# Where the token order of packed attention groups is put right: in the product's operand read, or in the copy out of PSUM

## The chip, the cores and the metric

The kernel runs on one core of one Trainium2 chip. The metric is the device time of one execution in microseconds; a set of runs is judged by its median. TensorE does the matmuls, VectorE (DVE) and ScalarE (ACT) do everything that reads PSUM, GpSimd (POOL) issues the loads and does part of the normalisation, SyncE (SP) issues transposing DMAs and the stores.

## The reference

Chunked attention over 8 batches, 8 heads, 576 tokens of 64 elements, in chunks of 64 tokens that attend only to themselves, and then a multiplicative feed-forward network on the 4608 tokens of width 512:

```python
scores = scale * np.matmul(q_c, k_c.transpose(0, 1, 2, 4, 3))      # per chunk of 64 tokens
attn = np.exp(scores - max)                                        # softmax over the 64 keys
attn = attn / (attn.sum(axis=-1, keepdims=True) + 1e-09)
x = np.matmul(attn, v_c)                                           # -> [4608, 512], heads side by side
a = x @ w1                                                         # 512 -> 1024
b = x @ w2
out = ((a * b) @ w3) @ w_out                                       # 1024 -> 1024 -> 512
```

The inputs and the output are float32; the kernel computes in bf16 with float32 sums. It first folds w3 and w_out into one matrix.

## The kernel before, in words

**Groups.** The 72 chunks are taken two at a time, as 36 groups of 128 tokens. The steps of group g have short names: `qk` loads q and k (GpSimd), `t` turns them on TensorE into the bank `p_tr` (or `tq` turns them by a DMA from SyncE), `kc` and `q.0`, `q.1` copy them out, `s` makes the scores in the bank `p_sc`, `mx`, `sd`, `ex`, `sm`, `an` are the softmax, `at` turns the probabilities on TensorE (or `ta` by DMA), `ac` copies them to `at`, `av` multiplies them with v into the bank `p_av` (line 488), and `x` copies the product, cast to bf16, into `xt` (a CAST at line 275 on ACT or 277 on DVE). The banks `p_tr`, `p_sc`, `p_at` and `p_av` have one buffer each, so `av` of one group waits for `x` of the group whose `av` came before.

**Feed-forward.** Nine tiles of four groups each. `a3.5` and `b3.5` are the products of tile 3 with columns 5 of w1 and w2 (line 579, four matmuls each), `c3.5` copies a out of its bank (ACT), `m3.5` multiplies it with b (DVE, line 588), `o14` is the last product of group 14 (line 608), `y14` its copy, `z14` its store. Four banks called `ffn` serve all of these in turn. `wt`, `wc`, `wm`, `wr` fold w3 and w_out at the start. `a0.0` needs `x0` to `x3`, and `a1.0` needs `x4` to `x7`.

**Order.** `ORDER` holds the order of each engine's steps, written out by hand. A planner walks through them with a cost for each step only to interleave the five lists into one program; on its engine each step stays where the list has it. Neither `ORDER` nor the planner's costs is touched. The parts of the lists that matter here:

```
PE : ... s4 at2 wm5.0 t5 wm5.1 wm6.0 wm6.1 wm5.2 av1 wm5.3 at3 wm6.2 s5 av2 t6 wt3 av0 at4 wm6.3 wm3.0 av3 wm3.1 wm3.2 wm3.3 a0.0 ...
     ... a0.7 a0.6 b0.6 at7 av6 b0.7 av4 s9 t10 o2 av7 o1 av5 s10 o0 a1.0 a1.4 b1.4 at8 ... s11 av8 o3 b1.2 ... b1.3 s12 b1.5 ...
ACT: ... ac3 x2 x0 wr6 kc6 x3 q6.0 ex5 ...   ... x6 ex8 x7 ex9 y0 c1.0 ...
DVE: ... sm4 x1 an4 mx5 wr5 wc3 sd5 ...   ... m0.7 x4 mx9 kc10 sd9 q10.0 y2 q10.1 y1 x5 sm8 sm9 mx10 an8 ac8 ... ac9 x8 sm11 m1.2 q13.0 kc14 q14.0 m1.1 mx12 ...
```

**Packed groups.** The groups in `PACKED` load two neighbouring tokens into one partition (tokens 2x and 2x + 1 with q and k each, so that a DMA run is 512 bytes long). Where TensorE turns such a group (`packed and not turned`), its tokens come out in the order (r x): first the 32 even tokens, then the 32 odd ones. `PACKED` holds 0 to 8, and of its other members each one is turned by DMA, so this holds for the nine groups 0 to 8. The exponential writes the keys back into their own order (`as_read`: bf16 writes that step over every second element). The queries stay in the order (r x) as columns of `at`, and `av_emit` puts them right: as the moving operand of its eight matmuls it reads column 0, 32, 1, 33 and so on, so that the bank `p_av` holds the tokens in order and `x_copy` reads and writes in one run.

Of the kernel before, what the change touches and what calls it, by code (L numbers as in the profile page):

```python
# [195 lines left out]
def kernel(  # L196
# [19 lines left out]
    nc = tc.nc  # L216
    B, H, S, D = q.shape
    C = 64
# [4 lines left out]
    P = 128  # L223
# [21 lines left out]
    def ps(tag, shape, dt=f32):  # L245
        return psum.tile(shape, dt, tag=tag, name=tag, bufs=BUFS[tag])
# [10 lines left out]
    xts = [wpool.tile([P, NM, TT], bf, tag=f"xt{i}", name=f"xt{i}") for i in range(3)]  # L257
    firsts = [sum(TILES[:i]) for i in range(len(TILES))]
# [3 lines left out]
    vds = [wpool.tile([P, NM, NCH, 2 * D], bf, tag=f"vd{i}", name=f"vd{i}") for i in range(BUFS["vd"])]  # L262
# [5 lines left out]
    def copy(eng, o, i, f=None):  # L268
        if f is not None:
            if eng == "ACT":  # L270
                nc.scalar.mul(o, i, f)
            else:
                nc.vector.tensor_scalar(o, i, f, None, op0=ALU.mult)
        elif eng == "ACT":
            nc.scalar.copy(o, i)  # L275
        else:
            nc.vector.tensor_copy(o, i)  # L277
# [105 lines left out]
    def add_group(g):  # L383
        box = {}
# [4 lines left out]
        turned, packed, by_head = TURN_QK[g], g in PACKED, g in EXP_8  # L389
# [90 lines left out]
        def av_emit(eng):  # L480
            t = box["av"] = ps("p_av", [P, NM, 2, C])
            for cc, (b, c) in enumerate(bc):
                for m in range(NM):
                    y, u = divmod(m, 2)
                    at = box["at"][:, 2 * cc + y, u * C:(u + 1) * C]
                    if packed and not turned:
                        at = at.rearrange("p (r x) -> p x r", r=2)
                    nc.tensor.matmul(t[:, m, cc, :], vds[b % len(vds)][:, m, c, :], at, start=True, stop=True)  # L488

        def x_copy(eng):  # L490
            i = tile_of[g]
            copy(eng, xts[i % len(xts)][:, :, (g - firsts[i]) * P:][:, :, :P], box["av"].rearrange("p m cc t -> p m (cc t)"))

        got = raws[g]["ops"]
        if turned:
# [21 lines left out]
        else:  # L517
            at = plan.add(f"at{g}", 0.23, at_emit, after=(an,), takes=("p_at",), uses=[(an, "an")], lag=0.2)
            ac = plan.add(f"ac{g}", {"DVE": 0.415, "ACT": 0.587}, at_copy, after=(at,), takes=("at",), uses=[(at, "p_at")])
        batches = sorted({b for b, _ in bc})  # L520
        av = plan.add(f"av{g}", 0.24, av_emit, after=[ac] + [o for b in batches for o in v_got[b]], takes=("p_av",),
                      uses=[(ac, "at")] + [(v_got[b][0], "vd") for b in batches], lag=0.2)
        x_done[g] = plan.add(f"x{g}", {"ACT": 0.586, "DVE": 0.688}, x_copy, after=(av,), uses=[(av, "p_av")])


# [172 lines left out]
```

## Time and profile before

| | before |
|---|---|
| median of 3 runs | 253.96 us (253.04 to 253.96) |
| the profiled execution: its own time | 254.97 us |
| its span, first to last instruction | 253.2 us |
| TensorE clock granted in it | 1.00 |
| PE busy | 240.3 us (95%) |
| DVE busy | 177.5 us (70%) |
| ACT busy | 132.6 us (52%) |
| POOL busy | 120.3 us (48%) |
| `av` matmuls (line 488) | 288 in 36 groups |
| `x` copies | 23 on ACT, 13 on DVE |

The page of a profile has the busy time of each engine, the span in 40 slices with the busy tenths of each, the chain of work that ended last followed back from the end, and the groups of instructions by line, engine and shape. In rows of the timeline and of the chain the columns are start and length in us, engine, line, and the operation with out<-in; in brackets stands how long the engine had been idle before it, and what ended that. A matmul's row in the timeline includes its way through the array, so neighbouring rows overlap; in the chain each row is counted from the end of the one before.

### The profile page before, as it was taken

How to read it: one execution, taken by the hardware profiler on the slowest of the kernel's cores; microseconds unless marked ns; L12 is line 12 of the kernel's file. 1: busy time of each engine (PE TensorE's matmuls, PEld its weight loads, DVE VectorE, ACT ScalarE, POOL GpSimd, SP SyncE). 2: the span in 40 equal slices, each digit the busy share in tenths (PEclk: the TensorE clock that was granted, in tenths of full speed). 3: DMA queues.
4: the chain of work that ended last, by engine and by line, in shares of the span. 5: the costliest groups of instructions: out<-in, count | busy, mean ns of one | idle time of the engine just before them, and what ended most of it. 6: DMA issues, size and time to landing. Idle time of an engine off the chain costs nothing.

```text
span 253.2 us, 4848 instructions
## 1 busy us (share of the span) xinstructions
PE 240.3 (95%) x1803; PEld 125.8 (50%) x1836; DVE 177.5 (70%) x334; ACT 132.6 (52%) x280; POOL 120.3 (48%) x148
## 2 busy tenths in 40 slices
PE   6777999999999999999999999999999999999994
PEld 2345565556455544644454454444554444444443
DVE  1388885898897997789894877699677576424331
ACT  5955866663555954652673195644567522331311
POOL 8778688994675496394694182800511001000000
PEclk9999999999999999999999999999999999999999
DMA  7999999999899999999999999999895260301755
GB/s 198 177 200 191 167 186 160 175 155 143 141 152 120 130 125 129 141 147 152 173 149 158 127 156 144 175 172 199 114 220 133 95 199 0 104 0 72 262 211 203
DMA packets 150167, 38.33 MB, mean 151 GB/s; under 512 B 139136, under 2 KB 144640, under 8 KB 150144
## 3 DMA queue, kind: packets, MB, share of 16 engines
q0 software_dynamic: 109216, 18.88, 97.9%
q1 hardware_dynamic: 40928, 19.14, 36.8%
q8 instruction: 14, 0.23, 0.4%
q14 instruction: 9, 0.07, 0.1%
HBM read 38.80 MB, written 9.44 MB: 191 GB/s over the span
## 4 chain that ended last, share of the span: by engine, by line
PE 75%; DMA 12%; ACT 4%; DVE 3%; POOL 3%; issue 2%; ACTq 0%; DVEq 0%; POOLq 0%; SPq 0%
PE ffn L579 42%; PE ffn L608 22%; PE p_av L488 4%; DMA raw<-in_k_dram 4%; DMA vd<-in_v_dram 4%; PE p_sc L432 3%; DMA wo_sb<-in_moe_w_out_dram 2%; DMA kqT<-raw 2%; ACT a_sb L275 2%; POOL raw L325 1%; PE p_at L474 1%; PE ffn L546 1%; DVE abT L588 1%; ACT xt L275 1%; DVE an L469 1%
## 5 line engine op out<-in xcount | busy, mean ns | idle before, releaser
L579 PE MATMUL ffn<-xt,w_sb 128*128 128x512 bf16 x556 | 132.8, 379 | 1.2 <-DVE abT L588 0.4
L579 PEld LDWEIGHTS <-w_sb 128*128 128x128 bf16 x576 | 53.4, 98 | 57.4 <-issue 0.7
L608 PE MATMUL ffn<-w3o_sb,abT 128*128 128x512 bf16 (+2 forms) x296 | 66.0, 367 | 0.4
L588 DVE TENSOR_TENSOR abT<-a_sb,ffn 128x512 bf16<-128x512 f32 x72 | 48.2, 679 | 19.6 <-PE ffn L579 14.4
L469 POOL TENSOR_TENSOR an<-e,rs 128x512 bf16<-128x512 bf16 x20 | 20.8, 1041 | 85.8 <-DVE rs L465 42.5
L275 ACT COPY a_sb<-ffn 128x512 f32<-128x512 f32 x72 | 41.5, 600 | 36.2 <-PE ffn L579 35.0
L608 PEld LDWEIGHTS <-abT 128*128 128x128 bf16 x304 | 28.5, 98 | 30.8
L440 DVE TENSOR_REDUCE nm<-p_sc 128x8 f32<-128x512 f32 x36 | 24.3, 675 | 10.5 <-PE p_sc L432 10.4
L463 DVE TENSOR_REDUCE ss<-e 128x8 f32<-128x528 bf16 x36 | 25.1, 696 | 8.8 <-ACT e L453 6.6
L453 ACT ACTIVATE e<-sd 128x512 bf16<-128x512 f32 x25 | 16.9, 677 | 21.7 <-DVE sd L444 18.1
L322 POOL DMA_DIRECT2D raw<-in_k_dram x30 | 26.0, 876 | 0.4 <-issue 0.4
L322 POOL DMA_DIRECT2D raw<-in_q_dram x30 | 25.8, 882 | 0.5 <-PE ffn L579 0.5
L459 ACT ACTIVATE e<-p_sc,nm 128x64 bf16<-128x64 f32 x88 | 19.4, 342 | 10.6 <-DVE nm L440 10.6
L275 ACT CAST xt<-p_av 128x512 bf16<-128x512 f32 x23 | 13.6, 590 | 11.3 <-PE p_av L488 11.2
L335 POOL DMA_DIRECT2D vd<-in_v_dram x16 | 18.9, 1190 | 0.0
L488 PEld LDWEIGHTS <-vd 128*128 128x128 bf16 x288 | 14.6, 98 | 8.0 <-issue 1.4
L277 DVE COPY o_sb<-ffn 128x512 f32<-128x512 f32 (+2 forms) x13 | 8.3, 635 | 14.4 <-PE ffn L608 11.6
L488 PE MATMUL p_av<-at,vd 128*128 128x64 bf16 x288 | 16.6, 201 | 0.8 <-ACT xt L275 0.3
L444 DVE TENSOR_TENSOR sd<-p_sc,nm 128x512 f32<-128x512 f32 x25 | 17.1, 683 | 0.3
L432 PEld LDWEIGHTS <-qd 128*128 128x128 bf16 x288 | 12.4, 98 | 8.1 <-DVE qd L277 1.9
L546 PE MATMUL ffn<-wo_sb,w3t 128*128 128x512 bf16 x60 | 15.4, 379 | 0.8 <-DMA wo_sb<-in_moe_w_out_dram 0.3
L275 ACT COPY o_sb<-ffn 128x512 f32<-128x512 f32 (+1 forms) x13 | 7.2, 566 | 13.1 <-PE ffn L608 13.1
(54 smaller groups left out, 202.4 us busy)
## 6 DMA issues: line engine op xcount, KB each, us to landing
out_dram<-o_sb SPq DMA_DIRECT2D x23, 256.0 KB, 2.5
vd<-in_v_dram POOLq DMA_DIRECT2D x16, 288.0 KB, 7.1
raw<-in_q_dram POOLq DMA_DIRECT2D x32, 128.0 KB, 5.9
raw<-in_k_dram POOLq DMA_DIRECT2D x32, 128.0 KB, 6.5
w_sb<-in_moe_w_dram POOLq DMA_DIRECT2D x16, 128.0 KB, 5.3
out_dram<-held_w SPq DMA_DIRECT2D x8, 256.0 KB, 2.7
w_sb<-in_moe_w_dram POOLq DMA_DIRECT2D x6, 256.0 KB, 7.3
stage<-in_moe_w_dram SPq DMA_DIRECT2D x2, 512.0 KB, 4.0
```

The costliest lines, as they stand in the source:

```text
L275: nc.scalar.copy(o, i)
L322: nc.gpsimd.dma_start(box["t"].rearrange("p (w h d) -> p w h d", w=2, h=H)[r, w], x.rearrange("h p d -> p h d"))
L335: nc.gpsimd.dma_start(vds[b % len(vds)][halves[t], :, :, t * D:(t + 1) * D].rearrange("p m c d -> p (m c) d"), v[b, NM * t:NM * (t + 1)].r ...
L432: nc.tensor.matmul(sc[:, cc, y, t, :], qd[:, s, cc, :], box["kT"][:, s, cc * C:(cc + 1) * C], start=True, stop=True)
L440: nc.vector.tensor_reduce(nm[:, :, 0], flat(box["sc"]), axis=AX.X, op=ALU.max, negate=by_head)
L459: nc.scalar.activation(o, j, ACT.Exp, bias=box["nm"][:, i, :])
L463: nc.vector.reduce_sum(ss[:], e[:], axis=AX.X)
L469: (nc.gpsimd if eng == "POOL" else nc.vector).tensor_mul(an[:], e[:, :, :C], box["rs"].to_broadcast([P, 8, C]))
L488: nc.tensor.matmul(t[:, m, cc, :], vds[b % len(vds)][:, m, c, :], at, start=True, stop=True)
L579: nc.tensor.matmul(t[:, :w], wt[:, ki, j * P:(j + 1) * P], x[:, ki, :], start=(ki == 0), stop=(ki == KO - 1))
L588: nc.vector.tensor_mul(box["abT"][:, j, :w], box["as", j][:, :w], box["b", j][:, :w])
L608: nc.tensor.matmul(t[:, :x1 - x0], box["abT"][:, ki, tk * P:(tk + 1) * P], w3o_sb[:, ki, x0:x1], start=(ki == 0), stop=(ki == FO - 1))
```

## The change

`av_emit` no longer reorders: for every group it reads the 64 columns of `at` in one run, as it already does for the other 27 groups. For the nine groups 0 to 8 the bank `p_av` then holds the tokens as (r x), and `x_copy` reorders: its output is written in one run as before, and its input is read from PSUM as token 0, 32, 1, 33 and so on, float32 elements 128 bytes apart. Of these nine copies, `x0`, `x2`, `x3`, `x6` and `x7` are on ACT, and `x1`, `x4`, `x5` and `x8` on DVE. No instruction is added or removed, and no order, wait or buffer is changed.

```diff
@@ av_emit, x_copy @@
                 for m in range(NM):
                     y, u = divmod(m, 2)
-                    at = box["at"][:, 2 * cc + y, u * C:(u + 1) * C]
-                    if packed and not turned:
-                        at = at.rearrange("p (r x) -> p x r", r=2)
-                    nc.tensor.matmul(t[:, m, cc, :], vds[b % len(vds)][:, m, c, :], at, start=True, stop=True)
+                    nc.tensor.matmul(t[:, m, cc, :], vds[b % len(vds)][:, m, c, :],
+                                     box["at"][:, 2 * cc + y, u * C:(u + 1) * C], start=True, stop=True)
 
         def x_copy(eng):
             i = tile_of[g]
-            copy(eng, xts[i % len(xts)][:, :, (g - firsts[i]) * P:][:, :, :P], box["av"].rearrange("p m cc t -> p m (cc t)"))
+            o, t = xts[i % len(xts)][:, :, (g - firsts[i]) * P:][:, :, :P], box["av"].rearrange("p m cc t -> p m (cc t)")
+            if packed and not turned:
+                o = o.rearrange("p m (cc x r) -> p m cc x r", cc=2, r=2)
+                t = t.rearrange("p m (cc r x) -> p m cc x r", cc=2, r=2)
+            copy(eng, o, t)
```

## The prediction

> **What bounds the kernel now.** I read the page first (busy shares, slices, chain), then PE's waits, then the chain and the timelines of PE, ACT and DVE between 32 and 80 us, where all nine groups of the change lie.
>
> ```profile
> span 253.2 us, 4848 instructions
> PE 240.3 (95%) x1803; PEld 125.8 (50%) x1836; DVE 177.5 (70%) x334; ACT 132.6 (52%) x280; POOL 120.3 (48%) x148
> PE   6777999999999999999999999999999999999994
> DVE  1388885898897997789894877699677576424331
> ACT  5955866663555954652673195644567522331311
> PE 75%; DMA 12%; ACT 4%; DVE 3%; POOL 3%; issue 2%; ACTq 0%; DVEq 0%; POOLq 0%; SPq 0%
> ```
>
> PE is busy in every slice from the fifth on, so TensorE sets the time, and its order is fixed: whatever it finishes earlier moves all that follows, unless it then has to wait. From 33 us to the end PE's list of waits has two rows:
>
> ```profile
> PE ffn L579 <- DVE abT L588: 0.4, 1, 0.4
> PE p_av L488 <- ACT xt L275: 0.3, 1, 0.3
> ```
>
> Both come late: the chain passes from PE through a transposing DMA to reach the second.
>
> ```profile
> 118.58 0.25 PE p_sc L432 x8
> 118.89 5.19 DMA kqT<-raw
> 126.69 0.39 PE p_av L488 x8
> ```
>
> That DMA starts when PE's scores have released a buffer, so an earlier PE starts it earlier too; I count what is gained before 80 us as kept. The slack of DVE and ACT is what must be looked at: in the slices between 38 and 82 us (DVE 8 8 9 7 9 9 7) DVE is close to PE.
>
> **The part removed: the stepped read of PE.** In the chain a group's eight `av` matmuls are one row. The nine groups run from 32.70 to 70.81; the first plain one is at 79.34.
>
> ```profile
> 32.70 0.67 PE p_av L488 x8
> 36.31 0.49 PE p_av L488 x8
> 70.81 0.49 PE p_av L488 x8
> 79.34 0.23 PE p_av L488 x8
> ```
>
> The same eight matmuls of the same size take 0.49 us with the stepped read and 0.23 with the plain one (the 0.67 of the first includes a pipe that had run empty). Each group frees 0.26 us of PE: nine make 2.34 us. That is the most there is to gain, 0.9%.
>
> **The part added: the stepped read of the copy.** Nine copies read float32 from PSUM in hops of 128 bytes. The trace has no such read. What it has:
>
> ```profile
> L275 ACT CAST xt<-p_av 128x512 bf16<-128x512 f32 x23 | 13.6, 590 | 11.3 <-PE p_av L488 11.2
> L277 DVE CAST xt<-p_av 128x512 bf16<-128x512 f32 x13 | 8.9, 684 | 3.5 <-PE p_av L488 3.5
> L275 ACT COPY o_sb<-ffn 128x512 f32<-128x512 f32 x12 | 7.0, 591 | 12.4 <-PE ffn L608 12.3
> L275 ACT COPY o_sb<-ffn 128x128 f32<-128x128 f32 x1 | 0.3, 267 | 0.7 <-PE ffn L608 0.7
> L277 DVE COPY o_sb<-ffn 128x512 f32<-128x512 f32 x11 | 7.5, 685 | 8.5 <-PE ffn L608 5.7 <-remote 2.8
> L277 DVE COPY o_sb<-ffn 128x128 f32<-128x128 f32 x1 | 0.3, 292 | 0.5 <-PE ffn L608 0.5
> 57.03 0.81 ACT L453 ACTIVATE e<-sd 128x512 bf16<-128x512 f32 x1
> 61.29 0.64 ACT L453 ACTIVATE e<-sd 128x512 bf16<-128x512 f32 x1
> ```
>
> Below, nothing: as many elements go through, so a gain is excluded, and the engine may take one word of any address per step. Above, each element costs twice its step: (591 - 267) / 384 = 0.84 ns on ACT, (685 - 292) / 384 = 1.02 ns on DVE, which over 512 elements is +0.43 and +0.52 us. Between them lie two measured steps. The exponential of a packed group (57.03), which writes with a step, takes 0.17 us longer than the plain one (61.29) for 512 elements. PE's stepped read costs 0.26 us for 8 x 64 = 512 columns, 0.51 ns each. I take +0.26 us per copy on both engines, because it is the very same hop moved to another reader; a doubling, +0.43/+0.52, is the upper end, nothing the lower.
>
> [...]
>
> **The sum, place by place.** Only what PE then waits for counts. No instruction is moved, so no queue is passed; but a longer copy holds up what is queued behind it on its engine, and the next `av`, which needs the bank.
>
> *Groups 1, 2, 0, 3 (32.7 to 39.5).*
>
> ```profile
> 36.84 0.59 ACT L275 CAST xt<-p_av 128x512 bf16<-128x512 f32 x1 [1.03 <-PE p_av L488]
> 37.49 0.59 ACT L275 CAST w3o_sb<-ffn 128x512 bf16<-128x512 f32 x1
> 37.98 0.59 ACT L275 COPY kT<-p_tr 128x512 bf16<-128x512 bf16 x1
> 38.45 0.61 ACT L275 CAST xt<-p_av 128x512 bf16<-128x512 f32 x1
> 37.73 0.66 PE L488 MATMUL p_av<-at,vd 128*128 128x64 bf16 x8
> 39.52 2.75 PE L579 MATMUL ffn<-xt,w_sb 128*128 128x512 bf16 x12
> 36.35 0.69 DVE L277 COPY w3t<-ffn 128x1024 bf16<-128x1024 bf16 x1 [0.33 <-PE ffn L535]
> ```
>
> PE earns 4 x 0.26 = 1.04 us by `a0.0` (39.52). `x0` (36.84) starts three products earlier, at 36.06, ends at 36.06 + 0.59 + 0.26 = 36.91; `av3` (37.73) now wants to start at 36.95 and just can. `wr6`, `kc6`, `x3` follow `x0` at the steps of these rows (the next starts 0.1 before an end, 0.49 and 0.47 apart): 36.81, 37.30, 37.77. `x3` ends at 37.77 + 0.61 + 0.26 = 38.64, and with 0.05 us for the release `a0.0` starts at 38.69, not at 39.52 - 1.04 = 38.48. Gain 0.83. `x1` on DVE pushes `an4`, `mx5`, `wr5` and `wc3` (36.35): it starts 0.26 earlier and lasts 0.26 longer, so this row of work stays where it was, `wc3` uses up its idle 0.33, and no product waits for it.
>
> *Groups 6, 4, 7 (55.9 to 60.6).*
>
> ```profile
> 56.55 0.59 ACT L275 CAST xt<-p_av 128x512 bf16<-128x512 f32 x1 [0.94 <-PE p_av L488]
> 57.21 0.66 PE L488 MATMUL p_av<-at,vd 128*128 128x64 bf16 x8
> 58.01 0.68 DVE L277 CAST xt<-p_av 128x512 bf16<-128x512 f32 x1
> 62.53 0.69 DVE L277 COPY held_w<-ffn 128x512 f32<-128x512 f32 x1 [0.95 <-remote]
> ```
>
> `x6` ends at 57.14, and `av4` starts at 57.21 behind it, in the only bank: 0.02 us of slack after the release. The 0.26 that `av6` frees is given back by `x6`'s 0.26; a gain of 0.02, that slack, remains. `av4` and `av7` free 0.26 each; `x4` (58.01) pushes what DVE does next, which has 0.95 us of idle before `y1` (62.53), and `x7` is followed on ACT by an idle stretch up to `y0`. Gain 0.52.
>
> *Groups 5 and 8.*
>
> ```profile
> 63.14 0.68 DVE L277 CAST xt<-p_av 128x512 bf16<-128x512 f32 x1
> 65.94 1.29 DVE L469 TENSOR_TENSOR an<-e,rs 128x512 bf16<-128x512 bf16 x1
> 67.38 0.39 PE L474 MATMUL p_at<-ident,an 128*128 128x128 bf16 x4
> 73.58 0.68 DVE L277 CAST xt<-p_av 128x512 bf16<-128x512 f32 x1
> 77.13 0.67 DVE L588 TENSOR_TENSOR abT<-a_sb,ffn 128x512 bf16<-128x512 f32 x1
> 78.09 1.03 PE L579 MATMUL ffn<-xt,w_sb 128*128 128x512 bf16 x4
> ```
>
> Behind `x5` (63.14) DVE has no idle up to `an8`, which ends at 67.23; `at8` takes it at 67.38, slack 0.1. `x5` itself follows `y1`, so `av5`'s faster end does not move it. PE's queue stands at `at8`: the 0.26 of `av5` is lost and 0.26 - 0.10 = 0.16 more. Behind `x8` (73.58) DVE is full up to `m1.1`, which ends at 77.80 and frees the bank that `b1.5` (78.09) takes: slack 0.24, so of `av8`'s 0.26 nothing is left and 0.02 is lost.
>
> Sum: 0.83 + 0.02 + 0.52 - 0.16 - 0.02 = 1.19 us, about 1.2. The profiled execution would take 254.97 - 1.2 = 253.8 us; it stands 1.01 above the median of the runs, 253.96, so the median comes to 252.8.
>
> **The rivals.**
>
> *The copies pay nothing for the hops.* ACT and DVE take one float32 per 0.84 and 1.02 ns, while PE's plain read takes a column every 0.23 / 512 = 0.45 ns; a memory that serves PE's hops at 0.49 / 512 = 0.96 ns would serve these readers at nearly their own pace. Then `a0.0` gains 1.04, groups 6, 4 and 7 give 0.78, and only the slacks of 0.10 at `at8` and 0.24 at `b1.5` bound groups 5 and 8, since DVE's work there does not end earlier of itself: -2.16 us, 251.8. Against it: ACT's stepped write at 57.03 costs 0.17 us, though ACT handles only one element per 0.84 ns there.
>
> [...]
>
> *The hop doubles the copy's element time* (+0.43 on ACT, +0.52 on DVE). Then `x3` ends 2 x 0.17 later than in my sum, and `a0.0` gains 0.83 - 0.34 = 0.49; `x6` costs 0.43 - 0.02 - 0.26 = 0.15; `av4` and `av7` still give 0.52; `at8` loses 0.52 - 0.10 = 0.42, `b1.5` 0.52 - 0.24 = 0.28. Sum: 0.16 gained, no change, 253.8.
>
> *Slower: each hop costs two further element times* (+0.86, +1.04). The place is the one bank `p_av` and the queues behind it. `x0` ends at 36.06 + 0.59 + 0.86 = 37.51, `x3` at 39.84, so `a0.0` starts 0.37 late; `x6` costs 0.86 - 0.28 = 0.58; `x4` exceeds its 0.95 by little, gain 0.43 for `av4` and `av7`; `at8` loses 0.94, `b1.5` 0.80. Sum 2.3 us slower, 256.2. It turns from gain to loss at about +0.46 on ACT and +0.56 on DVE. For it: the hop of 128 bytes is wider than any in the trace. Against it: PE's 64-byte hop only about doubles.
>
> That the change would leave the product's read stepped is no rival: its shape becomes that of the 79.34 row.
>
> **How the numbers follow.** No more than 0.5% (1.27 us) either way can be told from no change here: the three runs lie 0.36% apart. I give my forecast (+0.15 to +0.35 a copy, 252.2 to 253.2) 0.37, the free copies 0.24, the doubled ones 0.24, the dearer ones 0.15. Faster by over 0.5% are nearly all of the free case (0.23) and some 0.16 of my own: 0.39. Slower by over 0.5%: most of the dearest case and a little for waits that I have not seen, 0.15. The rest is 0.46. The range runs from the free case with the runs' own spread, 251.4, to 254.8, which takes in the doubled case and the beginning of the dear one.
>
> **What would show it.** Right: line 488 at 0.23 us a group everywhere in the chain; CAST rows `xt<-p_av` at about 0.85 us on ACT and 0.94 on DVE for groups 0 to 8, unchanged after 79 us; `a0.0` near 38.7; small new waits of PE at `av4` (on ACT `xt`) and at `at8` (on DVE `an`). CAST rows unchanged and `a0.0` at 38.5 show the free case; rows of 1.0 and 1.2 us the doubled one. It would be wrong if the gain by 80 us is there and then gone: then the loads or DMA transposes after 100 us hold PE back, which I excluded.

## The result, and the profile after

| | before | after |
|---|---|---|
| median | 254.18 us (20 runs) | 253.26 us (20 runs) |
| the profiled execution: its own time, span | 254.97, 253.2 us | 253.75, 252.0 us |

The ratio of after to before is 0.9946, with a 95% interval of 0.9921 to 0.9971: 1.4 us faster, between 0.7 and 2.0. The medians of all 20 runs differ by 0.9 us; the ratio leaves out one slow run on each side. The forecast was 1.2 us. The profile shows that the number came out right by luck, through two errors of opposite sign.

The page of after: its busy times, the shares of the chain of work, and two of its costliest groups (busy time and mean ns of one; behind the second bar the idle time before them):

```profile
span 252.0 us, 4881 instructions
...
PE 242.0 (96%) x1836; PEld 124.6 (49%) x1836; DVE 177.4 (70%) x334; ACT 132.3 (52%) x280; POOL 120.2 (48%) x148
...
PE 75%; DMA 10%; POOL 6%; ACT 4%; DVE 3%; issue 1%; POOLq 0%; ACTq 0%; DVEq 0%
...
L275 ACT CAST xt<-p_av 128x512 bf16<-128x512 f32 x23 | 13.5, 588 | 10.7 <-PE p_av L485 10.6
...
L277 DVE CAST xt<-p_av 128x512 bf16<-128x512 f32 x13 | 8.8, 680 | 3.4 <-PE p_av L485 3.4
```

PE's busy time is not to be compared with that of before: there 1803 of the 1836 matmuls are in the profile, here all of them.

The copies did not get longer: 588 and 680 ns on average, where they took 590 and 684. Nine of these 36 now read PSUM in hops. Single ones, in the timeline of ACT (start and duration of `x0`, its two followers and `x3`):

```profile
35.35 0.58 ACT L275 CAST xt<-p_av 128x512 bf16<-128x512 f32 x1 [0.77 <-PE p_av L485]
36.01 0.59 ACT L275 CAST w3o_sb<-ffn 128x512 bf16<-128x512 f32 x1
36.49 0.59 ACT L275 COPY kT<-p_tr 128x512 bf16<-128x512 bf16 x1
36.97 0.60 ACT L275 CAST xt<-p_av 128x512 bf16<-128x512 f32 x1
```

and in that of DVE (`x4`):

```profile
57.00 0.68 DVE L277 CAST xt<-p_av 128x512 bf16<-128x512 f32 x1
```

`x0` and `x3` read in hops, the two between them do not, and all four take the same. The products got as short as was said. What is new stands in the chain of work of after between 49 and 70 us (start and duration):

```profile
49.38 7.48 DMA raw<-in_k_dram
56.90 0.62 PE p_tr L403 x8
...
69.45 0.23 PE p_av L485 x8
```

and in its list of PE's waits from 32 us on (sum, count and longest, in us):

```profile
PE ffn L581 <- ACT a_sb L275: 0.7, 1, 0.7
PE p_av L485 <- DMA vd<-in_v_dram: 0.5, 1, 0.5
PE ffn L581 <- DVE abT L590: 0.4, 1, 0.4
PE p_tr L399 <- DMA raw<-in_k_dram: 0.3, 1, 0.3
```

Two of the four are waits for loads, at `t8` and `av6`, and a third load ends on the chain: group 10's k, issued at 49.38, lands at 56.85, and `t10` starts at 56.90. In the timeline of PE (for `a0.0`, `av6`, `t10`, `at8`, `av8`, `b1.5`):

```profile
37.88 2.75 PE L581 MATMUL ffn<-xt,w_sb 128*128 128x512 bf16 x12
...
55.10 0.39 PE L485 MATMUL p_av<-at,vd 128*128 128x64 bf16 x8 [0.53 <-DMA vd<-in_v_dram]
...
56.90 0.62 PE L403 MATMUL p_tr<-ident,raw 128*128 128x128 bf16 x8
...
66.01 0.40 PE L474 MATMUL p_at<-ident,an 128*128 128x128 bf16 x4
...
69.29 0.40 PE L485 MATMUL p_av<-at,vd 128*128 128x64 bf16 x8
...
76.47 1.03 PE L581 MATMUL ffn<-xt,w_sb 128*128 128x512 bf16 x4
```

Before, `t10` started at 57.94, 1.39 us after its load (56.55), as its timeline of PE has it:

```profile
57.94 0.61 PE L403 MATMUL p_tr<-ident,raw 128*128 128x128 bf16 x8
```

From there to the end both executions take the same to 0.2 us, although three shorter products lie behind `t10`. The stretch up to `av8` is 0.31 us shorter, and 0.8 us is lost at 111.36, where PE's chain passes through a transposing DMA (in the second fence PE's timeline):

```profile
105.41 4.65 DMA kqT<-raw
```

```profile
111.36 1.02 PE L581 MATMUL ffn<-xt,w_sb 128*128 128x512 bf16 x4 [0.67 <-ACT a_sb L275]
```

Of `av1`'s start, 32.01 against 32.70, 0.69 us is luck: up to there the two programs are the same. Before, `av1` waited for a load (v of batch 0, landed at 32.66); in this execution that load had landed at 31.41, 0.60 us ahead of `av1`.

### The profile page after: what moved, and what is told of

It is laid out like the page before. It is cut to its first block, busy times and chain, and to the rows that moved or that the text cites. A ratio compares the mean times of both kernels' runs of the same rounds, so it can differ in the third digit from the quotient of the medians.

```text
span 252.0 us, 4881 instructions
## 1 busy us (share of the span) xinstructions
PE 242.0 (96%) x1836; PEld 124.6 (49%) x1836; DVE 177.4 (70%) x334; ACT 132.3 (52%) x280; POOL 120.2 (48%) x148
## 4 chain that ended last, share of the span: by engine, by line
PE 75%; DMA 10%; POOL 6%; ACT 4%; DVE 3%; issue 1%; POOLq 0%; ACTq 0%; DVEq 0%
PE ffn L581 41%; PE ffn L610 25%; DMA raw<-in_k_dram 5%; PE p_sc L432 3%; PE p_av L485 3%; DMA w_sb<-in_moe_w_dram 2%; DMA kqT<-raw 2%; PE ffn L548 2%; POOL w_sb L344 1%; POOL raw L325 1%; ACT a_sb L275 1%; POOL raw L322 1%; POOL vd L335 1%; PE ffn L537 1%; DVE nm L440 1%
## 5 line engine op out<-in xcount | busy, mean ns | idle before, releaser
L581 PE MATMUL ffn<-xt,w_sb 128*128 128x512 bf16 x576 | 135.0, 379 | 1.0 <-ACT a_sb L275 0.7
L581 PEld LDWEIGHTS <-w_sb 128*128 128x128 bf16 x576 | 53.4, 98 | 58.2 <-issue 1.7
L610 PE MATMUL ffn<-w3o_sb,abT 128*128 128x512 bf16 (+2 forms) x304 | 66.8, 368 | 0.0
L548 PE MATMUL ffn<-wo_sb,w3t 128*128 128x512 bf16 x64 | 16.8, 387 | 0.9 <-ACT w_sb L275 0.9
L485 PEld LDWEIGHTS <-vd 128*128 128x128 bf16 x288 | 12.8, 98 | 7.8 <-issue 1.5
L485 PE MATMUL p_av<-at,vd 128*128 128x64 bf16 x288 | 14.3, 193 | 0.7 <-DMA vd<-in_v_dram 0.5
L275 ACT COPY qd<-kqT 64x512 bf16<-64x512 bf16 x16 | 9.8, 614 | 8.3 <-DMA kqT<-raw 8.0
```

The source lines that it names most:

```text
L548: nc.tensor.matmul(box["wp"][:], box["t"][:, ki, :], wo_sb[:, ki, :], start=(ki == 0), stop=(ki == FO - 1))
L581: nc.tensor.matmul(t[:, :w], wt[:, ki, j * P:(j + 1) * P], x[:, ki, :], start=(ki == 0), stop=(ki == KO - 1))
L610: nc.tensor.matmul(t[:, :x1 - x0], box["abT"][:, ki, tk * P:(tk + 1) * P], w3o_sb[:, ki, x0:x1], start=(ki == 0), stop=(ki == FO - 1))
```

## The experiments

**Two theories.** *Loads:* copies are free, nine products free 2.3 us, but TensorE, once faster, meets the loads of v1 and of group 10's k, which landed no earlier in after (54.97 and 56.85 us) than in before (54.50 and 56.55); about a microsecond goes there. *PE only:* all of it is there at 80 us, and is lost to waits behind 100 us or was never more than the runs' spread.

All times were compared with runs of the kernel before on the same chip. This table has what I read off the traces (start of a step in us; "k10" is the landing of group 10's k):

| kernel | ratio to before (95%) | av1 | k10 | t10 | t10 after k10 | av1 to av8 | av8 to end |
|---|---|---|---|---|---|---|---|
| before | 1 | 32.70 | 56.55 | 57.94 | 1.39 | 37.94 | 182.53 |
| after | 0.9946 (0.9921 to 0.9971) | 32.01 | 56.85 | 56.90 | 0.05 | 37.28 | 182.69 |
| after_again | 0.9950 (0.9923 to 0.9977) | 33.08 | 57.58 | 57.62 | 0.05 | 36.93 | 181.85 |
| cut_early | 0.9955 (0.9926 to 0.9985) | 32.49 | 56.27 | 56.32 | 0.05 | 36.21 | 181.85 |
| cut_late | 0.9925 (0.9894 to 0.9957) | 33.10 | 58.19 | 58.23 | 0.05 | 37.52 | 181.11 |
| first_six | 0.9960 (0.9931 to 0.9989) | 33.19 | 56.86 | 56.95 | 0.09 | 36.47 | 182.31 |
| last_three | 0.9962 (0.9933 to 0.9991) | 31.78 | 57.12 | 57.16 | 0.05 | 37.77 | 182.06 |
| write_step | 0.9936 (0.9908 to 0.9963) | 32.68 | 56.08 | 56.53 | 0.44 | 36.22 | 182.08 |
| light_before | 0.9995 (0.9963 to 1.0028) | 32.29 | 53.07 | 57.52 | 4.45 | 37.94 | 182.41 |
| light_after | 0.9907 (0.9870 to 0.9944) | 31.34 | 52.58 | 55.07 | 2.49 | 36.10 | 181.84 |
| order_loads | 0.9917 (0.9885 to 0.9950) | 31.15 | 55.16 | 56.66 | 1.49 | 36.16 | 181.86 |
| order_loads_b | 0.9916 (0.9884 to 0.9948) | 32.02 | 56.11 | 57.88 | 1.78 | 36.52 | 181.85 |
| order_loads2 | 0.9957 (0.9932 to 0.9982) | 33.02 | 57.25 | 58.63 | 1.38 | 37.80 | 181.45 |

Three stretches do not hold the same work as the others: cut_early lacks 0.86 us of products between `av1` and `av8`, cut_late lacks as much behind `av8`, and order_loads2 has the eight matmuls of `o3` (about 1.7 us) ahead of `av8` and not behind it. But for the ratios, each row is one execution.

**after_again: the changed kernel once more.**

> The changed kernel as it is, to stand beside the next three on one chip. Loads theory: the copies of groups 0 to 8 cost 0.59 us on ACT and 0.68 on DVE as before, nine products free 2.34 us of TensorE, and what is freed before t10 (56.9) is cut off where the loads land, at fixed times (raw k of group 8 at 46.5, v1 at 55.0, raw k of group 10 at 56.9), so that about 1.0 to 1.1 us of the first six groups' 1.56 is kept and most of the 0.78 behind t10: ratio 0.993 to 0.996. PE-only theory: the whole 2.16 us is there at 80 us and is lost to later waits: same ratio, but PE without waits for loads between 42 and 57.

Ratio 0.9950, as expected of both. PE's waits from 33 us on decide for loads:

```profile
PE p_av L485 <- DMA vd<-in_v_dram: 0.6, 1, 0.6
PE p_tr L403 <- DMA raw<-in_k_dram: 0.6, 1, 0.6
PE ffn L581 <- DVE abT L590: 0.4, 1, 0.4
```

The two largest are loads. This time `av1` itself waited 0.6 us for v of batch 0 (33.08), and `t10` 0.6 for group 10's k. The first wait stands ahead of all that the change frees, so the second alone speaks for the loads; it ends at 57.62, just behind the stretch that I had named (42 to 57). The wait for ACT `a_sb`, 0.7 us in the profile of after, is not there: in this execution the lines behind 100 us are not where the gain went.

**cut_early and cut_late: the same 0.86 us of TensorE taken out on either side of the loads.** Two products are summed over half of their inputs.

```diff
-                    for ki in range(KO):
+                    n_k = KO // 2 if (i, j) in ((0, 6),) else KO      # cut_late: ((7, 3),)
+                    for ki in range(n_k):
...
-                                         start=(ki == 0), stop=(ki == KO - 1))
+                                         start=(ki == 0), stop=(ki == n_k - 1))
```

> The changed kernel, with a0.6 and b0.6 summed over half of the 512 inputs only (two of four matmuls each left out, 0.86 us of TensorE), just ahead of av6. Loads theory: av6 still starts when v1 has landed (about 55.0) and t10 when group 10's k has (56.9); the 0.86 us turn into waits and the time is that of the changed kernel within 0.2 us. PE-only theory: 0.86 us less than the changed kernel (ratio to before 0.991).

> The changed kernel, with the same 0.86 us of TensorE left out of a7.3 and b7.3 (about 200 us). Loads theory and PE-only theory both: TensorE sets the time there, 0.7 to 0.9 us less than the changed kernel (ratio to before 0.991). If it were unchanged too, then something other than TensorE's order would bound the whole kernel.

0.9955 for the early cut, against 0.9950 uncut: nothing gained. The late cut gives 0.9925; the intervals of the two overlap, but the traces say it sharply: from `av8` to the end it takes 181.11 us, where the uncut kernel and cut_early take 181.85. The late cut is kept to 0.74 of 0.86 us. From `av1` to `av8` cut_early takes 36.21 us, 0.72 less than after_again, but group 10's k landed 1.31 us earlier in this execution, and `t10` started 1.30 earlier with it. The early cut ends up here, in the chain of work of cut_early and, in the second fence, in its timeline of PE:

```profile
49.00 7.27 DMA raw<-in_k_dram
56.32 0.62 PE p_tr L403 x8
```

```profile
54.20 0.40 PE L474 MATMUL p_at<-ident,an 128*128 128x128 bf16 x4 [0.43 <-DVE an L469]
```

Half of it goes to a wait for `an7` on DVE, which I had not foreseen, so this cut does not test the loads alone; and `t10` again starts 0.05 us after its load landed. In these executions TensorE's time ahead of `t10` is worth nothing by then; its time behind it is worth nearly what it measures (0.74 of 0.86 us).

The changed work ahead of `av8` is whole in cut_late, and its waits from 33 us on are a third sample of it:

```profile
PE p_tr L403 <- DMA raw<-in_k_dram: 0.6, 1, 0.6
PE p_av L485 <- DMA vd<-in_v_dram: 0.4, 1, 0.4
PE ffn L582 <- DVE abT L591: 0.4, 1, 0.4
```

Here `t10` and `av6` (55.88) wait for loads, 1.0 us together.

**first_six and last_three: the change in parts, ahead of `t10` and behind it.**

```diff
+                    if packed and not turned and not (g in (0, 1, 2, 3, 4, 6)):      # last_three: (5, 7, 8)
+                        at = at.rearrange("p (r x) -> p x r", r=2)
...
-            if packed and not turned:
+            if packed and not turned and (g in (0, 1, 2, 3, 4, 6)):
```

> Only the groups ahead of t10 (0, 1, 2, 3, 4, 6) are changed; 7, 5 and 8 keep the stepped product and the plain copy. Loads theory: t10 starts within 0.1 us of the landing of group 10's k, as in the changed kernel, so of 1.56 us about 1.0 is kept; from t10 to the end it takes 195.0 us, 0.78 more than in the changed kernel (194.2). Ratio 0.995 to 0.998. PE-only theory: t10 waits for nothing, all of 1.56 is kept, ratio 0.994.

> Only the groups behind t10 (7, 5, 8) are changed. Loads theory: t10 starts a microsecond or more after the landing of group 10's k, as in the kernel before, and the 0.78 us behind it are kept but for 0.1 to 0.2 at at8: from t10 to the end 194.2 us, ratio 0.997 to 0.998. PE-only theory: the same 0.6 to 0.78 us.

0.9960 and 0.9962: the parts are worth about 1.0 us each, between 0.2 and 1.8; last_three was expected to be worth less (0.997 to 0.998), and the intervals are too wide to say whether the parts add up to the whole. With first_six `t10` starts 0.09 us after its load and the rest takes 195.02 us, as expected. Not as expected, from `av1` to `t10` it takes 23.76 us, 1.48 less than before (25.24), and no load is in its list of waits: in this execution nearly all of the 1.56 us was kept, with `av1` late (33.19) and the load landing just ahead of `t10`. The other miss is in last_three. `t10` was to start a microsecond behind its load, and it did not, as PE's timeline of last_three has it:

```profile
57.16 0.62 PE L403 MATMUL p_tr<-ident,raw 128*128 128x128 bf16 x8
```

That is 0.05 us after the landing (57.12), with the stepped products still in all six groups ahead. In this execution `av1` had come early (31.78, v of batch 0 having landed at 31.14) and group 10's k late. So the kernel before is not clear of the loads either: its slack was 1.39 us in one execution, and in another, with the same work ahead of `t10`, there was none.

**write_step: the step on the other side of the copy.** PSUM is read in one run and bf16 written to every second element.

```diff
-                o = o.rearrange("p m (cc x r) -> p m cc x r", cc=2, r=2)
-                t = t.rearrange("p m (cc r x) -> p m cc x r", cc=2, r=2)
+                o = o.rearrange("p m (cc x r) -> p m cc r x", cc=2, r=2)
+                t = t.rearrange("p m (cc r x) -> p m cc r x", cc=2, r=2)
```

> The plain product, and a copy that reads PSUM in one run and writes bf16 with the step (every second element), the other way to mend the order. If the step is dear only where SBUF is written or read, the copies grow by about 0.17 us on ACT (0.76 us), as the packed exponential does against the plain one, and by something like it on DVE (0.75 to 0.85), while a step read from PSUM is free. If they stay at 0.59 and 0.68, a step is free for a copy on either side. By the prediction's sum the longer copies cost 0.5 us of the gain, but since loads cap the first six groups only about 0.2 to 0.3 us more than the changed kernel.

The timelines of write_step, in a fence each, of ACT (`x2`), DVE (`x4`) and PE (`av6`, `av4`):

```profile
34.67 0.74 ACT L275 CAST xt<-p_av 128x512 bf16<-128x512 f32 x1 [0.31 <-PE p_av L485]
```

```profile
57.00 0.72 DVE L277 CAST xt<-p_av 128x512 bf16<-128x512 f32 x1
```

```profile
54.85 0.40 PE L485 MATMUL p_av<-at,vd 128*128 128x64 bf16 x8
...
56.06 0.39 PE L485 MATMUL p_av<-at,vd 128*128 128x64 bf16 x8
```

A step costs a copy something where it writes: 0.15 us on ACT, about as expected, but only 0.04 on DVE, where 0.07 to 0.17 was expected. It shows in one place of the sum: from `av6` to `av4` it is 1.21 us, not 1.10 as in after_again, since `x6` is 0.15 longer and there is next to no slack. The total, 0.9936, does not differ from the changed kernel's; such 0.15 us are mostly covered. In this execution no load was waited for behind `av1`: `t10` had 0.44 us, and from `av1` to `av8` it took 36.22 us with all the loads, 1.72 less than before.

**light_before and light_after: the loads made lighter, with and without the change.** Four transfers of 128 KB, columns of w1 and w2 that are loaded ahead of v of batch 1, are left out in both, and the products that need them use the columns ahead of them, so that TensorE's work is the same.

```diff
-    for j in range(0, FO, 2):
+    for j in range(0, FO - 2, 2):
         load_w12(j, j + 2)
+    w12_got[6] = w12_got[7] = w12_got[5]
...
-                        nc.tensor.matmul(t[:, :w], wt[:, ki, j * P:(j + 1) * P], x[:, ki, :],
+                        nc.tensor.matmul(t[:, :w], wt[:, ki, (j - 2 * (j > 5)) * P:][:, :P], x[:, ki, :],
```

> The kernel before without the loads of the last quarter of w1 and w2 (four transfers of 128 KB between those of groups 8 and 9); the products that need these columns use the columns ahead of them instead, so the work of TensorE is the same. v1 and group 10's k should land some 2.5 us earlier, at about 52 and 54. Loads theory: stepped products leave TensorE mostly behind the loads, so little changes: from av1 to av8 37.8 to 38.0 us, ratio to before 0.997 to 1.000.

> The changed kernel without the same loads. Loads theory: t10 now starts at least 0.5 us after group 10's k has landed, av6 after v1, from av1 to av8 it takes 35.9 to 36.2 us (37.9 less eight times 0.26), and the gap to light_before is the whole 1.9 to 2.2 us: ratio to before 0.990 to 0.993. If the time stays that of the changed kernel (0.995), the loads were not what held it back.

Ratios 0.9995 and 0.9907. The loads of v of batch 1 and of group 10's k land 3.4 and 3.5 us earlier than before (expected: 2.5). Lighter loads alone give nothing; the change on top of them gives 0.9%, 2.2 us, with an interval of roughly 1.0 to 3.5, as an estimate from the two intervals of the table. That overlaps with the 0.7 to 2.0 us with all loads, so the times alone do not show that the loads cost anything; the traces have to. `t10` in PE's timeline of light_before, then in that of light_after, and in the third fence all of PE's waits in light_after from 33 us on:

```profile
57.52 0.61 PE L403 MATMUL p_tr<-ident,raw 128*128 128x128 bf16 x8
```

```profile
55.07 0.61 PE L403 MATMUL p_tr<-ident,raw 128*128 128x128 bf16 x8
```

```profile
PE ffn L581 <- DVE abT L590: 0.4, 1, 0.4
```

No load is waited for. From `av1` to `av8` it takes 37.94 and 36.10 us: 1.84 less, where eight products give 2.08 and `at8` was expected to keep 0.16. In the changed kernel with all its loads the same stretch took 36.93, 37.28 and 37.52 (after_again, after, cut_late): 0.8 to 1.4 us more, in the three executions whose lists show waits for loads. It is not so in each: write_step, with the same products and all its loads, took 36.22, 0.1 us more.

**order_loads, order_loads_b and order_loads2: other matmuls put in front of the waits.**

```diff
-  ... s7 t8 a0.4 a0.5 b0.5 ... av4 s9 t10 o2 av7 ...      PE
+  ... s7 a0.4 t8 a0.5 b0.5 ... av4 s9 o2 t10 av7 ...
-  ... mx9 kc10 sd9 ...                                    DVE
+  ... mx9 sd9 kc10 ...
```

> The changed kernel with t8 moved behind a0.4 and t10 behind o2 on TensorE, and kc10 behind sd10's predecessor sd9 on DVE. Loads theory: the waits at t8 (0.34 us) and t10 (0.2) vanish because other matmuls are there to fill them; the one at av6 grows by up to the 0.34, so 0.2 to 0.5 us less than the changed kernel. PE-only theory: no change, within 0.1 us.

> order_loads once more, for its interval: 0.990 to 0.995 to before; as t8 and t10 have other matmuls ahead of them, no wait for a load over 0.5 us at these two.

0.9917 and 0.9916 on two occasions: clearly faster than before, by some 2.1 us. `t10` now starts 1.5 and 1.8 us behind its load, and of the second run's waits this is all that is left:

```profile
PE ffn L581 <- DVE abT L590: 0.4, 1, 0.4
PE p_av L485 <- DMA vd<-in_v_dram: 0.2, 1, 0.2
```

By the ratios that is 0.7 to 0.9 us less than the changed kernel, more than the 0.2 to 0.5 expected; the intervals overlap with 0.9950's, so that it beats the changed kernel is likely but not shown.

order_loads2 went further: `av6` behind `b0.7`, and `o3` brought forward as a filler.

> order_loads, and av6 behind b0.7, av4 behind o2, o3 ahead of a1.0 (y3, ex9, sd9, y2 and x4 moved to suit), so that TensorE has other matmuls to do until v1 and group 10's k have landed. Loads theory: no wait for loads between 42 and 60 us whatever the run; 0 to 0.5 us less than order_loads on the median and less spread. Against it: o3 no longer fills the stretch behind av8, where DVE is full, so b1.5 and its neighbours may wait 0.3 to 1 us.

0.9957, which is 0.4% above order_loads; the intervals overlap, so that it is slower is likely but not shown. No load is in its list of waits, as expected. The filler had been covering DVE where it is full (in after, 9.69 of the 9.95 us from 66.45 to 76.40), and PE now waits 0.53 us for the bank there (its timeline):

```profile
75.87 1.02 PE L581 MATMUL ffn<-xt,w_sb 128*128 128x512 bf16 x4 [0.53 <-DVE abT L590]
```

## Why the prediction was right, and where it was not

**The part removed** was right: 0.49 us a group became 0.23, and with lighter loads about 2.2 us come through (roughly 1.0 to 3.5), where nine products make 2.34.

**The price of the copies** was wrong: +0.26 us, because it was "the very same hop moved to another reader", against none measured (588 and 680 ns on average, 590 and 684 before). This is the term of the sum that was mis-sized. The first rival, free copies (0.24 by my chances), is what happened, with the argument I had put beside it: the hop of TensorE costs 0.96 ns, ACT and DVE take a word only every 0.84 and 1.02 ns, all three worked out from rows of before. Whether that is the reason no run shows: by it ACT's copy would have grown by 0.12 x 512 = 61 ns, and it did not; and TensorE's hops are in SBUF, those of the copies in PSUM. The stepped exponential that I held against it (0.17 us) is a stepped write, and write_step shows that it is the write that costs: 0.15 us on ACT and 0.04 on DVE.

**"I count what is gained before 80 us as kept"** was wrong too, and it is the step that failed in kind: I looked for slack in DVE and ACT, and not in the landing times of the loads. In the trace of before `t10` had 1.39 us and `av6` 1.35 us behind their loads, readable then, against the 1.56 us that six free copies bring ahead of `t10`. That much would have cost the sum only 0.2 us; the rest of what was lost comes of the loads and `av1` falling otherwise in each execution, which one trace could not show. With free copies the sum should have been -2.16 us, less the 0.8 to 1.4 lost at the loads in three executions. That the measured 1.4 us lies 0.2 from the forecast is luck, and within the interval of the measurement.

**A row misread.** The digits 8 8 9 7 9 9 7 that I gave for DVE between 38 and 82 us are those of 57 to 101 us; between 38 and 82 the row has 5 8 9 8 8 9 7. Nothing in the sum rests on them.

**Places of the sum.** `at8` has the slack that I gave it: in after it comes 4.96 us behind `av5`, in before 5.05, where 4.79 would be without a wait, so 0.17 is lost there even with free copies. `a0.0` came 1.53 us behind `av3` instead of 1.79, so there was no wait for `x3`. The forecast of waits behind `x6` fails with the price, but its slack was right, as write_step shows. The DMA transposes behind 100 us, which I had excluded, held PE back in one execution: of the nine executions with the whole change, six take 181.84 to 182.08 us from `av8` to the end (before: 182.53), cut_late about as much less as was cut, order_loads2 has other work there, and only after takes more (182.69), with the wait for ACT `a_sb` of 0.7 us that no other shows. It fell into the very profile that stands beside the result.

**A wait that comes and goes.** From `av8` to the end it takes 0.57 us less in light_after than in light_before, where the sum has 0.24 for `av8`. Nearly all of the rest stands at `av19`, the product at 126.69 in the trace of before, whose wait for `xt` the prediction shows. From `av18` to `av19` it takes 1.10 us when there is no wait, as in light_after (121.69 to 122.79), after and after_again, 1.41 in light_before (124.75 to 126.16) and 1.53 in before (125.16 to 126.69). I had taken this wait to move along with PE. That the change removes it is not shown: write_step has 1.34 there, cut_late 1.24, and first_six and last_three 1.10.

**Left open** is what makes v of batch 0 and group 10's k land earlier or later, and what decides on the wait at `av19`.

## What to carry to other kernels

When an edit frees time on the engine that sets the end, list what is next to bind at each place ahead: also the loads, by the time from each landing to its first use, and not only the other engines' idle. A slack towards a load, read from one execution, is one draw: here it was 1.39 us in one and nothing in another. A reordering read is worth trying at the reader that is slowest per element, as it was here (0.84 ns on ACT and 1.02 on DVE, worked out from the o_sb copies of before, against TensorE's 0.45 ns a column); that this holds for other shapes is not shown. A step on the read side and one on the write side have to be priced apart: here nothing against 0.15 us on ACT and 0.04 on DVE.

## What the runs showed of the hardware that was not expected

- A float32 read from PSUM in hops of 128 bytes cost ACT and DVE nothing (0.585 and 0.681 us for 512 elements), while TensorE's moving operand in hops of 64 bytes took 0.49 us for what takes 0.23 in one run.
- A bf16 write to every second element of SBUF cost a copy of 512 elements 0.15 us on ACT and 0.04 on DVE.
- With the same loads in the same order, group 10's k landed between 55.2 and 58.2 us in the eleven profiles that have all loads; that is more than the whole change. Part of it is the issue, which lies between 47.5 and 49.9 us; from issue to landing it took 7.0 to 8.5 us, and with the issue at 49.4 to 49.5 (five profiles) it landed between 56.5 and 57.6.
